# Windowed attention, soft routing and a feed-forward layer on one core: the last 64 tokens of every batch as two full-shaped units behind the others

## The chip, the cores and the metric

The kernel runs on one core of a Trainium2 chip. The metric is the device time of one execution in microseconds (us), lower is better. A time is given as the median of several executions. A profile is one execution recorded by the hardware profiler; its span runs from the first to the last instruction.

## The reference

Three layers follow each other, in float32, on 4 batches of 576 tokens (2304 tokens of 512 channels, 8 heads of 64):

```python
# 1. attention: each token sees itself and the 63 before it
mask = (rel >= 0) & (rel < 64)            # rel = query position - key position
attn = softmax(where(mask, q @ k.T / 8, -1e9))
x = (attn @ v)                            # -> (2304, 512)

# 2. soft routing: 8 experts x 4 slots, F = 1024
logits = x @ phi                          # (2304, 32)
d = exp(logits - logits.max(0)); d /= d.sum(0) + 1e-9    # over all tokens
slot_input = d.T @ x                      # (32, 512)
slot_out[e] = relu(slot_input[e] @ w1[e]) @ w2[e]
c = exp(logits - logits.max(1)); c /= c.sum(1) + 1e-9    # over the 32 slots
x = c @ slot_out

# 3. feed-forward, 2048 wide
h = x @ w_in
out = (h * sigmoid(1.702 * h)) @ w_out
```

## The kernel before

**Attention** is a software pipeline over a list `work` (L295). A unit is one pair of heads of one batch: 128 partitions hold the two heads, 64 channels each. The first 512 tokens of a batch, for one pair of heads, are a full unit (16 in all, `u`): four column blocks `c`, each of two chunks of 64 queries `j`, each chunk against 128 keys. The last 64 tokens of a batch, for all four pairs of heads together, are a half unit (4 in all, one per batch, standing second in its batch): two column blocks. So there are 20 steps `i`, in the order full, half, full, full, full for each batch.

A step (loop at L608) emits, for TensorE in this order: the scores of item i (`emit_s`: mask products L315, score products L329), the turn of the probabilities of item i-1 (`emit_t`, L350, copied to SBUF by ScalarE at L351), what the batch's routing has to do early, the turn of the attended rows of item i-2 (`xt_step`, L406 for a full unit, L412 for a half one), the value products of item i-1 (`emit_pv`, L365), and what routing has to do late. ScalarE computes the exponentials of a full item in two groups of four (`emit_e`, L341); VectorE takes the row maxima (L334) ahead of them and normalizes item i-1 behind the value products (`emit_norm`, L375 to L391).

**Routing** runs over batches as a running softmax over tokens, each batch 576 tokens in five tiles (four of 128 and one of 64, `TB`). For a batch it is spread over four steps: `logits` (L467, in two parts of 256 and 320 tokens), `lsum` (L480, two parts, four partial sums added by a product with a tiled identity), `lmax` and `dexp`, `dtr` (two turns of five blocks each, L510), `slots` (four products of 128 tokens, L527, and two of 64, L532), `gather` (running sum), and the softmax over slots (`c_max` to `c_mul`, on VectorE ahead of `emit_norm`). The last batch's routing stands behind the loop (L677 to L734) and ends with the 32 slot inputs turned (L731), which the expert layer waits for.

**Conversion** of six weight blocks that arrive as 64-bit words (`narrow_a` on ScalarE, `narrow_c` on GpSimd, `narrow_b` on VectorE, L169 to L177) is spread over steps 2 to 16; it stands at the end of a step.

**Loads** all go through one queue, SP's, in program order: q and k of a full unit (`load_qk`, 512 KB, three buffers), v (`load_v`, 256 KB, three buffers), the half unit's q, k and v of a batch (`load_sg`), and the expert weights (`load_w`, 1 MB each, 32 of them, one for each step from the third on, `W_AT`). The first 16 weight blocks go to buffers of their own, the next seven into the memory of the attention stage (`arena`) as it comes free, the last nine into buffers that the first expert products free. GpSimd scales q by 1/8 (`scale_q`, L218) and copies v for the second chunk (`shift_v`, L238, L241).

**Then** the expert layer (`emit_w1` L746, `emit_w2` L786) reads the 32 weight blocks, with the combine weights turned beside it (`c_last` for the four 64-token tiles, L448), and the feed-forward layer (L942 to L995) takes the rest of the span.

Of the kernel before, what the change touches and what calls it, by code (L numbers as in the profile page):

```python
# [32 lines left out]
W_AT = {i: 1 for i in range(2, 18)}  # L33
W_AT.update({18: 3, 19: 1})
# [8 lines left out]
TB = 5  # L43
# [7 lines left out]
SG0 = 0  # L51
X0 = SG0 + 4 * 192 + 517
QK0 = X0 + 2560
V0 = QK0 + 2048
MASK0 = V0 + 2 * 904
IDB0 = MASK0 + 512
XT0 = IDB0 + 64
LT0 = XT0 + 4 * S
D0 = LT0 + S
PHI0 = D0 + 160  # L60
X1 = PHI0 + 128
ARENA = 7 * 2048
N_E = 16
LS0 = NE * 260 + 512 - S

FP = 4

PERM = list(range(9))


def tw(t):
    return 128 if t < 4 else 64


@with_exitstack
def attention_softmoe_ffn(
# [4 lines left out]
    sg: bass.AP,  # L81
# [39 lines left out]
    lg = [cst.tile([128, TB, NS], F32, name=f"lg{b}") for b in range(B)]  # L121
# [4 lines left out]
    wof = cst.tile([128, N_WO, 512], F32, name="wof")  # L126

# [9 lines left out]
    plan += [(w2t, w2, i, 16 - N_E + i if i < N_E - 9 else None) for i in range(16)]  # L137
# [64 lines left out]
    vi = [v[:, 1:904].rearrange("p (i d) -> p i d", d=129) for v in vb]  # L202

    sgb = mem(SG0, 768).rearrange("p (u k) -> p u k", u=NHP)
    sgv = mem(SG0 + 768, 517)
# [3 lines left out]
    xb = [mem(o, 2560).rearrange("p (t d) -> p t d", t=TB) for o in (X0, X1)]  # L209
    xT = mem(XT0, KD * S).rearrange("p (k n) -> p k n", k=KD)  # L210
    lt = mem(LT0, S)
    phi4 = mem(PHI0, 128)

    def load_qk(u):
        nc.sync.dma_start(out=qkb[u % 3], in_=qk[u])

    def scale(q, eng):
# [3 lines left out]
    def scale_q(u, eng):  # L221
        scale(qkb[u % 3][:, 0:512], eng)

    def load_v(u):
        nc.sync.dma_start(out=vi[u % 3][:, 0:4, 0:128], in_=vt[u])

    def load_sg(b):
        nc.sync.dma_start(out=mem(SG0, 768), in_=sg[b, :, 0:768])
        nc.sync.dma_start(
            out=sgv[:, 1:517].rearrange("p (u d) -> p u d", u=NHP)[:, :, 0:128],  # L230
            in_=sg[b, :, 768:1280].rearrange("p (u d) -> p u d", u=NHP))

    def scale_sg(eng):
        scale(sgb[:, :, 0:64], eng)

    def shift_v(u):
        vd = vi[u % 3]
# [8 lines left out]
    for i in range(3):  # L246
        nc.vector.memset(vb[i][:, 0:1], 1.0)
        nc.vector.memset(vi[i][:, 0:4, 128:129], 1.0)
# [213 lines left out]
    def routing(b):  # L462
# [112 lines left out]
        def c_hi():  # L575
            c_high(b * S, st["pq"])
# [562 lines left out]
```

## Time and profile before

| | before |
|---|---|
| time, median of 3 executions (lowest to highest) | 387.69 us (387.28 to 388.26) |
| span of the profiled execution | 385.5 us |
| attention steps, first scores to the end of the loop's last full step | 6.4 to 104.2 us |
| turn, products and routing behind them, to the first expert product | 104.2 to 120.4 us |
| expert layer | 120.4 to 153.2 us |
| feed-forward layer to the end | 153.2 to 385.5 us |
| TensorE busy / ScalarE busy / VectorE busy (whole span) | 367.9 / 202.4 / 244.1 us |

The profile lists the busy time of each engine, the span in 40 equal slices, the groups of instructions by line, the chain of waits that ended last, and the instructions in order of time. PE is TensorE's matmul, PEld its weight load, DVE VectorE, ACT ScalarE, POOL GpSimd, SP the engine that issues the transfers. A float32 product shows as two records. A matmul's recorded duration overlaps with its neighbours', so the cost of a group on TensorE is read as the distance from its start to the start of the next group.

### The profile page before, as it was taken

The page shows a single profiled execution, that of the slowest core. Times are in us where ns is not written, and L with a number is a line of the kernel's source. Part 1 is how long each engine was busy: PE and PEld are TensorE (multiplying, and loading weights), DVE is VectorE, ACT ScalarE, POOL GpSimd, SP SyncE. Part 2 cuts the span into 40 slices and gives each one's busy share as a digit, 9 for nine tenths or more (in the row PEclk, how much of TensorE's full clock was granted, in tenths as well). Part 3 has the DMA queues.
Part 4 walks back from the last instruction along what each step waited for, and adds up shares of the span by engine and source line. Part 5 has one row for each costly group of instructions (what it writes and reads, how often), then busy time and mean ns, then how long its engine had stood idle before and what let it go on. Part 6 is the DMA issues. An engine that isn't in the chain of part 4 may idle for free.

```text
span 385.5 us, 7973 instructions
## 1 busy us (share of the span) xinstructions
PE 367.9 (95%) x3128; PEld 277.4 (72%) x3128; DVE 244.1 (63%) x554; ACT 202.4 (52%) x517; POOL 47.4 (12%) x79
## 2 busy tenths in 40 slices
PE   6999989889989999989999999999999999999995
PEld 5787667677654333768877888788887888888884
DVE  3466696896743540386677669597968795362624
ACT  2598868788742320556475745455444553343330
POOL 5335465343010000000000000000000000000000
PEclk9699999999999999999999999999999999999999
DMA  8999999999568999231413141313110000021304
GB/s 275 334 354 385 396 384 397 376 385 382 227 265 295 401 418 387 91 110 57 163 43 103 31 151 57 109 54 111 54 54 2 1 0 2 1 94 71 153 12 164
DMA packets 26726, 70.84 MB, mean 184 GB/s; under 512 B 2496, under 2 KB 13760, under 8 KB 22720
## 3 DMA queue, kind: packets, MB, share of 16 engines
q1 hardware_dynamic: 26688, 70.33, 49.3%
q8 instruction: 25, 0.41, 0.4%
q14 instruction: 13, 0.11, 0.1%
HBM read 65.60 MB, written 4.72 MB: 182 GB/s over the span
## 4 chain that ended last, share of the span: by engine, by line
PE 81%; DVE 9%; ACT 8%; issue 1%; POOL 0%; ACTq 0%
PE s L969 17%; PE t L969 16%; PE v L969 16%; PE m L942 4%; PE s L746 4%; PE v L786 4%; PE v L365 3%; PE s L329 3%; ACT pa L341 3%; PE m L350 3%; ACT pa L351 3%; DVE nm L334 1%; PE s L315 1%; PE v L256 1%; PE m L471 1%
## 5 line engine op out<-in xcount | busy, mean ns | idle before, releaser
L929 ACT ACTIVATE r<-m 128x384 fp32r<-128x384 f32 x96 | 47.3, 494 | 83.2 <-PE m L942 83.2
L956 DVE TENSOR_TENSOR r<-g,r 128x384 fp32r<-128x384 f32 x96 | 51.2, 553 | 50.6 <-ACT g L929 42.3
L969 PE MATMUL t<-w,r 128*128 128x512 f32 x288 | 75.9, 395 | 0.0
L969 PE MATMUL s<-w,r 128*128 128x512 f32 x288 | 74.9, 394 | 0.4 <-DVE r L956 0.4
L969 PE MATMUL v<-w,r 128*128 128x512 f32 x288 | 73.3, 389 | 0.0
L969 PEld LDWEIGHTS t<-w,r 128*128 128x128 f32 x288 | 53.8, 188 | 14.9 <-issue 3.7
L969 PEld LDWEIGHTS v<-w,r 128*128 128x128 f32 x288 | 54.1, 188 | 11.4
L969 PEld LDWEIGHTS s<-w,r 128*128 128x128 f32 x288 | 52.5, 188 | 9.5 <-DVE r L956 0.9
L341 ACT ACTIVATE pa<-s,nm 128x128 f32<-128x128 f32 x144 | 42.6, 401 | 11.7 <-DVE nm L334 11.6
L929 ACT ACTIVATE g<-m 128x384 f32<-128x384 f32 x96 | 47.7, 498 | 0.0
L334 DVE TENSOR_REDUCE nm<-s 128x4 f32<-128x512 f32 (+1 forms) x40 | 23.5, 629 | 6.0 <-PE s L329 5.8
L942 PE MATMUL m<-cT,w 128*128 128x384 f32 (+2 forms) x112 | 26.0, 322 | 0.6 <-ACT g L929 0.6
L351 ACT COPY pa<-m 128x512 f32<-128x512 f32 (+1 forms) x40 | 20.2, 563 | 9.9 <-PE m L350 9.6
L942 PEld LDWEIGHTS m<-cT,w 128*128 128x128 f32 x112 | 20.7, 188 | 5.8 <-ACT g L929 1.7
L350 PE MATMUL m<-ident,pa 128*128 128x128 f32 x144 | 21.8, 291 | 0.2 <-ACT pa L341 0.2
L350 PEld LDWEIGHTS m<-ident,pa 128*128 128x128 f32 x144 | 16.3, 145 | 4.5 <-issue 2.1
L365 PE MATMUL v<-arena,pa 128*64 128x65 f32 x384 | 15.9, 227 | 0.9 <-ACT pa L351 0.4
L365 PEld LDWEIGHTS v<-arena,pa 128*64 128x64 f32 x384 | 13.0, 137 | 4.2 <-ACT pa L351 2.9
L375 DVE TENSOR_SCALAR rs<-v 128x4 f32<-128x4 f32 (+1 forms) x40 | 5.2, 157 | 16.8 <-PE v L365 16.7
L746 PE MATMUL s<-w,phis 128*32 128x512 f32 x128 | 14.5, 594 | 0.5 <-DVE phis L734 0.5
L329 PE MATMUL s<-arena 64*64 64x128 f32 x384 | 14.7, 285 | 0.1
L315 PE MATMUL s<-arena 64*64 64x512 bf16 (+1 forms) x80 | 10.2, 397 | 3.7 <-ACT pa L341 3.0
(184 smaller groups left out, 461.0 us busy)
## 6 DMA issues: line engine op xcount, KB each, us to landing
w<-in_w_dram SPq DMA_DIRECT2D x24, 1024.0 KB, 10.4
w<-in_w_out_dram SPq DMA_DIRECT2D x16, 512.0 KB, 3.3
arena<-in_w_dram SPq DMA_DIRECT2D x7, 1024.0 KB, 6.9
iraw<-in_w_in_dram SPq DMA_DIRECT2D x12, 512.0 KB, 3.3
arena<-in_qk_dram SPq DMA_DIRECT2D x10, 512.0 KB, 8.7
out_dram<-w SPq DMA_DIRECT2D x16, 256.0 KB, 2.1
rawt<-in_qk_dram SPq DMA_DIRECT2D x6, 512.0 KB, 7.1
arena<-in_vt_dram SPq DMA_DIRECT2D x10, 256.0 KB, 7.4
```

The costliest lines, as they stand in the source:

```text
L329: nc.tensor.matmul(st[h][rows[j], c, :], q, k, start=False, stop=(c == n - 1), tile_position=(64 * h, 64 * j))
L334: nc.vector.tensor_reduce(out=nm[:, h, 0:n], in_=st[h][:, 0:n], axis=AX.X, op=ALU.max, negate=True)
L341: nc.scalar.activation(out=pb[h][:, c, :], in_=st[h][:, c, :], func=ACTF.Exp, bias=nm[:, h, c:c + 1], scale=1.0)
L350: nc.tensor.transpose(tt[:, c, :], pb[h][:, c, :], ident)
L351: nc.scalar.copy(ab[h][:, 0:n], tt[:, 0:n])
L365: nc.tensor.matmul(pvt[i][h][64 * j:64 * j + 64, c, :], ab[h][:, c, 64 * j:64 * j + 64], v, start=True, stop=True, tile_position=(0, 64 * j))
L746: nc.tensor.matmul(ph[32 * j:32 * j + 32, :], siT[:, kk, :], w1t[4 * r + j][:, kk, :], start=(kk == 0), stop=(kk == KD - 1), tile_position ...
L786: nc.tensor.matmul(po[32 * j:32 * j + 32, c], ht[:, e * 256 + fc * 32:e * 256 + fc * 32 + 32], w2t[i][:, j, c], start=(i == 0), stop=(i == ...
L929: nc.scalar.activation(out=(gh, g)[part], in_=ph[:, 0:PIECE], func=ACTF.Gelu_apprx_sigmoid)
L942: nc.tensor.matmul(ph[:, c - a:c - a + m], mst[:, f * 128:f * 128 + 128], cT(c, m), start=True, stop=True)
L956: nc.vector.tensor_tensor(out=gl, in0=g, in1=gh.bitcast(F32), op=ALU.subtract)
L969: nc.tensor.matmul(accs[t], a[:, c], b, start=(first and k == 0), stop=(last and k == 2))
```

## The change

The four half units go. In their place two tail units stand at the end of `work`, steps 16 and 17, each with the last 64 tokens of two batches: all four pairs of heads are its four column blocks, the two batches its two chunks, so a tail unit has a full unit's shape. A batch's own routing now covers 512 tokens in four tiles, in one part instead of two; the 256 tail tokens are a fifth routing group behind the loop, in two tiles (`xl`, `tail_logits`, `pd`, `pl`), whose logits are made in one accumulation with `phi4` in full (four blocks) instead of partial sums. The two turns of a batch share one bank. `gather` and the softmax over slots move behind `emit_norm` (`post`), the conversion's VectorE parts move to the middle of a step, `xt_step` ahead of the early routing. The loop has 18 steps; the last item's turn and value products stand behind it, among the last batch's `lsum`, `lmax`, `dexp`, `slots`. The tails' q and k come as four loads of 384 KB through the unit buffers, the last one into memory that the third batch's rows leave free. The arena is laid out anew and the seven weight blocks enter it in another order. The combine weights of the tails are turned as two full tiles; tokens lie in the order 4 x 512, then 4 x 64, and the host puts the rows back.

```diff
-W_AT = {i: 1 for i in range(2, 18)}
-W_AT.update({18: 3, 19: 1})
+W_AT = {i: 1 for i in range(2, 15)}
+W_AT.update({15: 1, 16: 1, 17: 2})
...
-    work = []
-    for b in range(B):
-        n = [(NHP * b + k, None) for k in range(NHP)]
-        work += n[0:1] + [(None, b)] + n[1:]
+    work = [(u, None) for u in range(NU)] + [(None, t) for t in range(2)]
...
+        def logits():
+            lp = bank("m")
+            for kk in range(KD):
+                nc.tensor.matmul(
+                    lp[32 * kk:32 * kk + 32], phis[:, kk, :], xT[:, kk],
+                    start=True, stop=True, tile_position=(0, 32 * kk))
+            nc.scalar.copy(lt, lp)
...
         def lsum():
+            lp = bank("m")
+            nc.tensor.matmul(lp, i4m, lt, start=True, stop=True)
+            nc.scalar.copy(ls, lp)
...
-                    start=True, stop=(t > 1), tile_position=(0, 32 * t))
-            for t in range(2):
-                cols = slice(256 * t, 256 * t + 256)
-                nc.tensor.matmul(
-                    pa[32 * t:32 * t + 32, cols], d[0:64, 4, :], x[0:64, 4, cols],
-                    start=False, stop=True, tile_position=(0, 32 * t))
+                    start=True, stop=True, tile_position=(0, 32 * t))
...
-        n = 5 * b
-        late[n + 6] = main[0:1]
-        early[n + 7] = main[1:2]
-        late[n + 7] = main[2:4]
-        early[n + 8] = main[4:5]
-        late[n + 8] = main[5:7] + norm[0:3]
-        late[n + 9] = norm[3:7]
+        n = NHP * b
+        late[n + 5] = [logits]
+        if b == B - 1:
+            break
+        early[n + 6] = [lsum]
+        late[n + 6] = [lmax, dexp]
+        early[n + 7] = [lambda f=turn: f(0, 1), total]
+        late[n + 7] = [slots]
+        post[n + 7] = [gather] + norm[0:2]
+        late[n + 8] = norm[2:3]
+        post[n + 8] = norm[3:7]
...
+    for i in range(ns):
+        emit_s(i)
         if i:
             emit_t(i - 1)
+        emit_e(i, 0)
+        convert(i, True)
+        if i > 1:
+            xt_step(i - 2)()
         for f in early.get(i, ()):
             f()
...
+        emit_e(i, 1)
         for f in late.get(i, ()):
             f()
         if i:
             emit_norm(i - 1)
+        for f in post.get(i, ()):
+            f()
...
+        if i < NU - 1:
+            scale_q(i + 1, nc.gpsimd)
+        elif i < NU + 1:
+            for n in range(2):
+                scale_q(NU + 2 * (i + 1 - NU) + n, nc.gpsimd)
...
+        if i == NU - 1:
+            set_ones(NL - 1, nc.gpsimd)
+            load_qk(NL - 1)
+            load_v(NL - 1)
...
+    load_w(2)
+    emit_t(ns - 1)
+    lsum()
+    xt_step(ns - 2)()
     sides[0][0]()
+    emit_pv(ns - 1)
+    lmax()
+    dexp()
+    emit_norm(ns - 1)
+    load_w(1)
     sides[0][1]()
...
+    turn(0)
+    tail_logits(0)
     xt_step(ns - 1, True)()
+    slots()
...
+    tail_logits(1)
...
+    nc.scalar.activation(
+        out=ltt, in_=lpt, func=ACTF.Exp, bias=m, scale=1.0, accum_out=ss)
...
+    for t in range(2):
+        nc.tensor.transpose(pd[:, t, :], ltt[0:32, t * 128:t * 128 + 128], ident[0:32, 0:32])
+    nc.vector.tensor_copy(dt, pd)
...
+            nc.tensor.matmul(
+                pl[32 * g:32 * g + 32, HALVES[c]], dt[:, t, :], xl[:, t, HALVES[c]],
+                start=True, stop=True, tile_position=(0, 32 * g))
...
-    c_last()
+    for f in side(TM, 4 * MT, "m"):
+        f()
```

## Rows read from the trace of the kernel before

**Rows 1.** The page, span in 40 slices of 9.64 us: granted clock and transfer rate.
```profile
PEclk9699999999999999999999999999999999999999
...
GB/s 275 334 354 385 396 384 397 376 385 382 227 265 295 401 418 387 91 110 57 163 43 103 31 151 57 109 54 111 54 54 2 1 0 2 1 94 71 153 12 164
```

**Rows 2.** Busy time by stretch: us, then each engine (records), clock, DMA share, GB/s.
```profile
63.17:89.18 26.01, 23.73 (x411) 17.58 (x407) 20.49 (x60) 19.82 (x60) 10.97 (x17) 1.00 1.02 383
...
109.52:120.38 10.86, 8.96 (x137) 5.99 (x134) 7.12 (x23) 3.75 (x11) 1.78 (x1) 1.00 0.54 189
120.38:153.17 32.79, 32.79 (x350) 11.91 (x350) 10.47 (x30) 6.34 (x15) 0.16 (x1) 1.00 1.01 398
```

**Rows 3.** TensorE in order of time: start us, us, line, out<-in, records [idle before, releaser].
```profile
62.04 1.20 PE L471 MATMUL m<-arena,phis 128*32 128x256 f32 x16
63.17 0.41 PE L315 MATMUL s<-arena 64*64 64x512 bf16 x4
...
64.38 0.66 PE L350 MATMUL m<-ident,pa 128*128 128x128 f32 x4
64.87 1.27 PE L480 MATMUL m<-arena,i 128*128 128x256 f32 x4
65.98 0.60 PE L406 MATMUL m<-ident,arena 128*128 128x128 f32 x4
66.51 0.69 PE L365 MATMUL v<-arena,pa 128*64 128x65 f32 x16
67.12 0.41 PE L315 MATMUL s<-arena 64*64 64x512 bf16 x4
...
68.34 1.09 PE L350 MATMUL m<-ident,pa 128*128 128x128 f32 x8
...
84.24 0.56 PE L315 MATMUL s<-arena 64*64 64x256 bf16 x4
...
85.21 1.15 PE L350 MATMUL m<-ident,pa 128*128 128x128 f32 x8
...
95.56 0.46 PE L510 MATMUL m<-ident,arena 32*128 32x32 f32 x5
...
96.61 0.66 PE L412 MATMUL m<-ident,arena 128*128 128x128 f32 x4
97.19 1.15 PE L365 MATMUL v<-arena,pa 128*64 128x65 f32 x32
98.28 1.06 PE L527 MATMUL m<-arena 128*32 128x512 f32 x8
99.27 0.62 PE L532 MATMUL m<-arena 64*32 64x256 f32 x4
99.83 0.41 PE L315 MATMUL s<-arena 64*64 64x512 bf16 x4
```

**Rows 4.** TensorE's waits, 20 to 110 us: us in total, times, longest.
```profile
PE m L406 <- DVE arena L385: 1.3, 3, 0.5
PE s L315 <- ACT pa L341: 1.1, 1, 1.1
```

**Rows 5.** The page's groups, the exponentials: count | busy, mean ns | idle before, releaser.
```profile
L341 ACT ACTIVATE pa<-s,nm 128x128 f32<-128x128 f32 x144 | 42.6, 401 | 11.7 <-DVE nm L334 11.6
```

**Rows 6.** TensorE in order of time, the scores of the third item, early.
```profile
15.55 1.78 PE L329 MATMUL s<-arena 64*64 64x128 f32 x32
```

**Rows 7.** TensorE in order of time, end of the routing and the last combine tiles.
```profile
117.27 0.62 PE L532 MATMUL m<-arena 64*32 64x256 f32 x4
...
118.83 1.08 PE L731 MATMUL m<-i,acc 128*128 128x32 f32 x8
...
137.69 1.08 PE L430 MATMUL t<-ident,lg 128*32 128x128 f32 x32
```

**Rows 8.** In order of time: SP issues q and k of a unit, GpSimd scales it.
```profile
76.19 0.33 SPq L215 DMA_DIRECT2D arena<-in_qk_dram  x1
...
83.58 0.62 POOL L218 TENSOR_SCALAR arena<-arena 128x512 f32<-128x512 f32 x1 [3.80 <-DMA arena<-in_qk_dram]
```

More of the change, by code (lines that the diff above doesn't have):

```diff
@@ L42 @@
 NT = B * S
-TB = 5
+TM = 4
+MT = 128 * TM
 MASKED = -1.0e9
@@ L136, in attention_softmoe_ffn @@
     plan = [(w1t, w1, i, None if i < N_E else i - N_E) for i in range(16)]
-    plan += [(w2t, w2, i, 16 - N_E + i if i < N_E - 9 else None) for i in range(16)]
+    plan += [(w2t, w2, i, (0, 2, 3, 1, 4, 5, 6)[i] if i < 7 else None) for i in range(16)]
     plan.reverse()
@@ L339, in emit_e @@
         st, nm = est[i]
-        for c in range(shape_of(i)):
+        for c in range(4):
             nc.scalar.activation(
@@ L416, in evac @@
-        def evac():
-            if split:
-                nc.scalar.copy(o[:, HALVES[0]], ps[0])
-                nc.vector.tensor_copy(o[:, HALVES[1]], ps[1])
-            else:
-                nc.scalar.copy(o, p)
+        ps = [pt[:, c] for c in HALVES]
+        if split:
+            ps[1] = bank("m")[:, HALVES[0]]
+        for k in range(4):
+            if t is None:
+                b, kk = divmod(u, NHP)
+                src = xb[b % 2][:, k, kk * 128:kk * 128 + 128]
+            else:
+                src = xl[:, t, k * 128:k * 128 + 128]
+            nc.tensor.transpose(ps[k // 2][:, 128 * (k % 2):128 * (k % 2) + 128], src, ident)
@@ L422, in xt_step @@
+        def evac():
+            if t is None:
+                nc.scalar.copy(xT[:, kk], pt)
+                return
+            o = xlT[:, :, 128 * t:128 * t + 128]
+            if not split:
+                nc.scalar.copy(o, pt.rearrange("p (k n) -> p k n", k=KD))
+                return
+            for k, copy in ((0, nc.scalar.copy), (2, nc.vector.tensor_copy)):
+                copy(o[:, k:k + 2], ps[k // 2].rearrange("p (k n) -> p k n", k=2))
         return evac
-    PARTS = ((0, 256), (256, S))
@@ new lines, in attention_softmoe_ffn @@
+    nc.vector.tensor_scalar(out=rsl, in0=rsl, scalar1=1e-9, scalar2=None, op0=ALU.add)
+    nc.vector.reciprocal(out=rsl, in_=rsl)
+    i4s = cst.tile([128, NS], F32, name="i4s")
+    nc.vector.tensor_scalar(
+        out=i4s, in0=i4m[:, 0:NS], scalar1=rsl, scalar2=None, op0=ALU.mult)
+    siT = phis
+    sides[2][0]()
+    psi = bank("m", (128, KD, 32))
+    for k, c in enumerate(HALVES):
+        p = slice(64 * k, 64 * k + 64)
+        nc.vector.tensor_tensor(out=acc[p, c], in0=pl[p, c], in1=acc[p, c], op=ALU.add)
+        for kk in (2 * k, 2 * k + 1):
+            nc.tensor.matmul(
+                psi[:, kk, :], acc[:, kk * 128:kk * 128 + 128], i4s, start=True, stop=True)
@@ L772, in attention_softmoe_ffn @@
     emit_ht(1)
-    for f in sides[3]:
+    for f in side(0, 3 * MT, "m"):
         f()
```

470 lines of the change are left out of this document (197 added, 273 removed).

## Prediction

> **What bounds the kernel now.** I read the span by stretches first [rows 2]. In one batch of the attention loop (five steps, 26.0 us) TensorE is busy for 23.7 us, VectorE for 20.5, ScalarE for 19.8: TensorE sets the pace, with 2.3 us of gaps, but ScalarE is not far behind. The expert layer is TensorE alone: 32.8 of 32.8 us. The feed-forward layer behind it is not touched (the order of the tokens changes, not the tiles' shapes), so only attention, routing and the expert layer can move. Transfers come next [rows 1]: 376 to 397 GB/s from the fourth to the tenth slice, then a dip, then 400 again: the first 96 us stream without a pause, and the question is whether a shorter loop overtakes its loads. The granted clock falls to 6 tenths in the second slice alone [rows 1]. Then I read TensorE in order of time [rows 3], taking the distance from one start to the next as a group's cost, and last its waits [rows 4].
>
> **Half units to tail units.** From [rows 3]: a half unit's scores take 85.21 - 84.24 = 0.97 us, its turn of probabilities 64.87 - 64.38 = 0.49, its turn of rows 97.19 - 96.61 = 0.58, its value products 67.12 - 66.51 = 0.61: 2.65 us, four times 10.60. A full unit costs 68.34 - 67.12 = 1.22 for scores, twice 0.49 for the turn, 66.51 - 65.98 = 0.53 for rows, 98.28 - 97.19 = 1.09 for value products: 3.82. Two tail units have its shapes: 7.64. The turn and score groups cost nearly as much for two column blocks as for four, so joining two saves. **-3.0 us**, all on TensorE, which has next to no gap in which it could have been hidden.
>
> **Routing of the first three batches.** 512 columns for 576 and one part for two: logits 63.17 - 62.04 = 1.13, times 512/576 = 1.00; lsum 65.98 - 64.87 = 1.11, becomes 0.99; the two turns 96.61 - 95.56 = 1.05 for ten blocks, 0.84 for eight; slots loses its second part, 99.83 - 99.27 = 0.56 [rows 3]. That is 1.0 us a batch, **-3.1 us**. ScalarE and VectorE lose their second copies and the 64-row pieces with it; I count nothing for them here.
>
> **The first steps.** The second step was a half unit and becomes a full one, in the stretch at half clock. At that clock 32 score products take 1.78 us [rows 6], the same group some 1.0 later. Half a unit's scores, turn and value products, about 1.2 us at full clock, stand where they cost twice: between 0 (the wait for the first exponentials there hides part) and +1.2; I take **+0.6 us**.
>
> **Behind the loop.** Before the last value products, TensorE now has the whole of the last batch's logits and lsum (1.00 + 0.99 us, where three quarters of the logits stood, 0.85) and the first combine turn, moved forward (1.0 for 32 records [rows 7]): +2.1. The 1.0 leaves the next stretch, where it is hidden today, so it is paid here; but the turn of the last probabilities, which now follows a step without scores and waits for its exponentials, gets the logits ahead of it as cover. I give that and what else overlaps an estimate of -1.4, between 0 and -2.1. **+0.7 us.** Behind the last value products lie 10.86 us now [rows 2], a serial chain: normalize, turn, logits, maximum, exponential, turn, slots, sum, turn. On the tails alone it has one exponential and one maximum of 256 columns instead of two each (-0.9, about two ScalarE and VectorE operations of 0.4 to 0.5), and the product behind the exponential is 0.56 us like slots' second part instead of 1.55 for both parts (99.83 - 98.28) [rows 3]: -1.0. From slots' second part to the last turn pass 118.83 - 117.27 = 1.56 us [rows 7]; the rescaling is now split over `i4s` and may add 0.2. The last batch's own slots (0.99) are queued on TensorE ahead of the second tail's logits, while the turned rows are copied: +0.1 for what outlasts that copy. Sum **-1.6 us**, between 0 and -2.5.
>
> **Expert layer.** The combine turns of four 64-token tiles become two full ones: 32 records take 1.08 us [rows 7], 16 half of it; the last batch's turn has six blocks for five, +0.1. **-0.4 us**, as TensorE has no gap there [rows 2].
>
> **Waits.** The 2.3 us of gaps a batch [rows 2] have two kinds of row: the turn of rows waits for VectorE's normalizing (1.3 us in all) and a score product waits for a bank that ScalarE's late exponentials hold (1.1) [rows 4]. Both are late because VectorE has the routing's softmax ahead of normalizing, and conversion ahead of the next maxima. The change moves the first behind and the second to where VectorE waits for the value products anyway: this can give back up to all 2.3 us a batch, 6.8 in three. Against it: every step is now a full one for ScalarE. A full unit's exponentials are 8 x 42.6/144 = 2.4 us [rows 5], and 19.8 us a batch of four such units and a half one [rows 2] leave some 4 for a full step with its copies and its share of routing. Steps that also convert and carry lsum and the batch's exponential need more than TensorE's time; by about 1.0 us in one step of four, I estimate. The half units were where ScalarE caught up. Bounds: -4.3 (nearly two thirds of the gaps) to +3.0 (that 1.0 each batch, nothing gained). I take **-1.5 us**, nearer the middle of them than the good end, because the chain rows show VectorE's lateness only in two steps of a batch.
>
> **Transfers.** The bytes up to the sixteenth weight block are the same (about 35 MB), in about the same time: at the end of my step 8 some 19.7 MB are asked for and, by [rows 1], about 18 delivered; by step 15 delivery has caught up. So nothing is added. The weight blocks for the arena are issued in step with what the routing frees, as before, and the nine behind them wait for expert products as before; they move ahead with the loop. Cover lost would show as gaps in the expert layer.
>
> **Sum.** -3.0 - 3.1 + 0.6 + 0.7 - 1.6 - 0.4 - 1.5 = -8.3. The profiled span is 385.5, so the new span would be 377.2; 2.2 us lie between span and median, so 387.69 - 8.3 = **379.4 us**. Own range of this case: 376.4 to 383.
>
> **A new load late in the loop.** The last tail's q and k are issued only after the third batch's slots have been read (step 15), scaled by GpSimd in step 16 and needed at the start of step 17, some 4 us after the issue. SP is in order, so the last v and the weight blocks 14 to 16 queue behind it. At 76.19 us a load of this kind was issued that GpSimd got at 83.58, 7.4 us later, but behind queued weight blocks [rows 8]. By my count little is queued at step 15, and 384 KB at 390 GB/s are 1.0 us. [...] The row of 7.4 us speaks for the queue as the larger part.
>
> **Rivals.** (1) ScalarE takes over: with only full steps, waits grow by the +3.0 instead of falling by 1.5. Time 379.4 + 4.5 = 383.9. For it speaks its 19.8 us busy a batch, of which only some 2 go with the half unit (four of its exponentials are 1.2) while the batch shrinks by about 4; against it, that the heavy step is followed by a step heavy for TensorE (turns and slots). (2) Slower: the late load above. From 4 us after its issue each us of delay is a us of TensorE's idle time; at 7.4 us it costs 3.4 (382.8); from 12.3 the whole gain is gone; at 14 the kernel is at about 389.4. For it: the loop is shorter and weight blocks come one a step, so the queue may hold two of them more than I count, and TensorE's clock could fall in so long a gap. Against it: it needs nearly twice the delay that the row shows. (3) No change: the half steps' TensorE time was cover for ScalarE and VectorE, and what TensorE saves is given back as waits everywhere: 387.7. Against it stands 23.7 us busy of 26.0. (4) Faster still: the granted clock is down in the second slice, which begins in the second step, where a score product waits for the first exponentials. If a full unit there keeps it at its upper level (2.4 GHz, not 1.2), the group of 1.78 us becomes 1.05 and its neighbours likewise, some 3 us: 376.4. The Trainium skill ("TensorE: Matmul & The Clock Gate", section "Part 1: The HAM clock gate") says that an idle stretch throttles the engine and sustained work releases it; the trace agrees (6 tenths in the second slice, 9 behind it), and by it this rival needs the gap to go. I see no reason for that: the same first exponentials end it.
>
> **How the numbers follow.** Chances: forecast 0.60, (1) 0.22, (2) 0.06, (3) 0.06, (4) 0.06. The range of 8 in 10 takes in the forecast's own and most of (1) and (4): 376.2 to 384.8. A measurement of this kernel tells about 0.3% (1.2 us) from no change. Faster by more: the forecast, (1) and (4), 0.88; within: 0.06; slower: 0.06.
>
> **What would show it.** In the profile after: the first expert product near 112.5 us instead of 120.4; a batch in four steps of together 21 to 21.5 us, with under 2 us of gaps on TensorE; from the last value products to the first expert product near 9.3 us; the expert layer still without a gap, 32.4 us long. Rival (1) shows as waits of the turn of probabilities or of a score product for ScalarE, 1 us and more in the lsum step; (2) as a wait of a score product for GpSimd at the start of step 17; (3) as batches of 25 us; (4) as a clock of 9 in all slices. Wrong would be the prediction above all if the gaps grow, since that term alone is an estimate of sign as well as size; the others are records that are no longer there.

## The result and the profile after

The changed kernel takes 375.14 us (median of four runs, 374.26 to 375.5) against 387.98 us for the kernel before, measured in turn with it. The ratio is 0.967, with a 95% interval of 0.962 to 0.972: 12.8 us faster, where 8.3 was forecast, and just under the low end of the range. The profiled span goes from 385.5 to 373.3 us, that is 12.2 less. The direction was right, the sizes of several terms were not; this section and the next ones look for the 4 us that came on top (4.5 by the medians, 3.9 by the spans).

The page of the changed kernel, granted clock and transfer rate in 40 slices of 9.33 us (compare [rows 1]):

```profile
PEclk9999999999999999999999999999999999999999
...
GB/s 237 338 387 392 388 393 391 388 361 317 420 419 421 420 391 277 56 114 112 59 112 56 103 67 113 58 86 83 114 0 0 2 0 0 2 122 48 138 34 169
```

The 6 in the second slice is gone, and the dip of 227 and 265 GB/s in the eleventh and twelfth slices has shrunk to one slice of 317.

Busy time by stretch of the changed kernel, columns as in [rows 2]. The stretches are the second and third batch, the one from the end of the loop to the end of the last value products, the one from there to the first expert product, and the expert layer:

```profile
26.39:46.84 20.45, 20.05 (x349) 14.74 (x347) 15.41 (x40) 17.04 (x51) 10.70 (x13) 1.00 1.04 391
46.84:67.78 20.94, 20.34 (x352) 14.72 (x348) 17.26 (x48) 17.70 (x54) 11.65 (x16) 1.00 1.05 390
95.86:100.32 4.46, 4.46 (x80) 3.46 (x79) 1.05 (x4) 3.63 (x9) 0.00 (x0) 1.00 1.02 419
100.32:109.27 8.95, 8.00 (x117) 5.92 (x116) 6.06 (x24) 2.96 (x9) 1.83 (x1) 1.00 1.02 421
109.27:141.71 32.44, 32.44 (x335) 11.55 (x335) 10.58 (x23) 6.12 (x11) 0.00 (x0) 1.00 1.02 411
```

Against [rows 2]: a batch takes 20.5 to 20.9 us instead of 26.0, and TensorE stands still for 0.4 and 0.6 us of it instead of 2.3. From the last value products to the first expert product it is 8.95 us instead of 10.86, and the expert layer takes 32.44 instead of 32.79, still without a gap. So the largest change is in the loop, and it is twofold: fewer records, and fewer gaps. (A wait inside a group, as in the logits below, counts as busy in these rows.)

TensorE in order of time in the changed kernel: the second step (first three lines), and the second batch (the rest):

```profile
9.67 0.40 PE L312 MATMUL s<-arena 64*64 64x512 bf16 x2 [1.76 <-ACT pa L339]
9.78 1.17 PE L327 MATMUL s<-arena 64*64 64x128 f32 x32
10.88 1.09 PE L347 MATMUL m<-ident,pa 128*128 128x128 f32 x8
...
30.44 1.60 PE L448 MATMUL m<-arena,phis 128*32 128x512 f32 x8
31.97 0.41 PE L312 MATMUL s<-arena 64*64 64x512 bf16 x4
...
34.37 0.60 PE L400 MATMUL m<-ident,arena 128*128 128x128 f32 x4
34.82 1.12 PE L457 MATMUL m<-arena,i 128*128 128x512 f32 x2
35.88 1.15 PE L362 MATMUL v<-arena,pa 128*64 128x65 f32 x32
```

Three readings. The second step still waits 1.76 us for the first exponentials (before: 1.86), but the full unit behind it then runs its 32 score products in 1.17 us, not in the 1.78 of [rows 6]. The logits, one part now, take 31.97 - 30.44 = 1.53 us where I had 1.00: the last quarter's weights wait for ScalarE's copy of the turned rows. And lsum takes 35.88 - 34.82 = 1.06, where I had 0.99.

ScalarE and TensorE's weight load (PEld) ahead of and in these logits, in order of time:

```profile
29.31 1.16 ACT L339 ACTIVATE pa<-s,nm 128x128 f32<-128x128 f32 x4
...
30.32 0.62 ACT L404 COPY arena<-m 128x512 f32<-128x512 f32 x1
...
31.00 0.14 PEld L448 LDWEIGHTS m<-arena,phis 128*32 128x32 f32 x2 [0.40 <-ACT arena L404]
```

The copy stands behind four exponentials of a full unit (1.16 us). In the kernel before, a half unit stood in that step: two exponentials (0.64 us), the copy from 35.33 to 35.94, and logits from 36.21 to 37.32 that didn't wait for it. In the next two batches of the changed kernel the logits take 1.85 and 1.86 us.

TensorE's waits in the changed kernel from 20 to 110 us, columns as in [rows 4]:

```profile
PE s L327 <- POOL arena L236: 1.2, 1, 1.2
PE m L400 <- DVE arena L381: 0.6, 2, 0.3
PE s L735 <- DVE phis L716: 0.5, 1, 0.5
```

The two waits of [rows 4] are answered by the second line: the turn of rows waits for VectorE 0.6 us in all instead of 1.3, and the wait of a score product for ScalarE's exponentials (1.1) is not in the list. New is the first line, which is the late load of the last tail's q and k. In order of time, SP, GpSimd and TensorE of the changed kernel:

```profile
84.66 0.33 SPq L228 DMA_DIRECT2D arena<-in_sq_dram  x1
...
90.00 0.40 POOL L236 TENSOR_SCALAR arena<-arena 128x256 f32<-128x256 f32 x1 [1.86 <-DMA arena<-in_sq_dram]
...
90.46 0.32 PE L327 MATMUL s<-arena 64*64 64x128 f32 x1 [1.22 <-POOL arena L236]
```

From issue to GpSimd 5.3 us pass, between the 1.0 that I took and the 7.4 of [rows 8].

### The profile page after: what moved, and what is told of

Read it like the earlier page. It is cut to its first block, busy times and chain, and to the rows that moved or that the text cites. A ratio compares the mean times of both kernels' runs of the same rounds, so it can differ in the third digit from the quotient of the medians.

```text
span 373.3 us, 7763 instructions
## 1 busy us (share of the span) xinstructions
PE 359.9 (96%) x3060; PEld 271.9 (73%) x3060; DVE 238.4 (64%) x520; ACT 200.1 (54%) x501; POOL 45.8 (12%) x74
## 4 chain that ended last, share of the span: by engine, by line
PE 82%; ACT 9%; DVE 5%; DMA 1%; issue 1%; POOL 0%; ACTq 0%
PE s L959 17%; PE t L959 17%; PE v L959 17%; PE m L932 4%; PE s L735 4%; PE v L776 4%; ACT pa L348 3%; PE v L362 3%; ACT pa L339 3%; PE s L327 3%; PE m L448 2%; PE m L347 2%; DMA arena<-in_sq_dram 1%; PE v L264 1%; PE m L507 1%
## 5 line engine op out<-in xcount | busy, mean ns | idle before, releaser
L332 DVE TENSOR_REDUCE nm<-s 128x4 f32<-128x512 f32 x36 | 23.1, 683 | 9.7 <-PE s L327 9.4
L348 ACT COPY pa<-m 128x512 f32<-128x512 f32 x36 | 19.5, 600 | 13.8 <-PE m L347 13.8
L347 PE MATMUL m<-ident,pa 128*128 128x128 f32 x144 | 19.7, 280 | 0.0
L347 PEld LDWEIGHTS m<-ident,pa 128*128 128x128 f32 x144 | 15.4, 141 | 3.8 <-issue 2.2
L327 PE MATMUL s<-arena 64*64 64x128 f32 x368 | 12.9, 269 | 1.2 <-POOL arena L236 1.2
L381 DVE TENSOR_TENSOR arena<-v,rs 128x256 f32<-128x256 f32 x36 | 13.6, 418 | 0.6
L904 ACT CAST w<-wf 128x512 fp32r<-128x512 f32 x14 | 8.7, 622 | 9.1 <-DVE wf L175 9.1
```

The costliest lines, as they stand in the source:

```text
L327: nc.tensor.matmul(st[h][rows[j], c, :], q, k, start=False, stop=(c == 3), tile_position=(64 * h, 64 * j))
L332: nc.vector.tensor_reduce(out=nm[:, h], in_=st[h], axis=AX.X, op=ALU.max, negate=True)
L347: nc.tensor.transpose(tt[:, c, :], pb[h][:, c, :], ident)
L348: nc.scalar.copy(ab[h], tt)
```

## The experiments

What was open: is the extra gain in the moves of the gather, the softmax and the conversion behind normalizing, put down as part of "waits" at 1.5 us; in TensorE's clock, charged with 0.6 us; or in a term of the records? Medians below stand beside those of the kernel before of the same comparison, which lie between 387.1 and 387.7 us unless they are given.

### The kernels again

Both kernels unchanged.

> The kernel before, unchanged, profiled a second time. Theory A (the clock's fall in the second slice belongs to the program: its second step is a half unit behind a pause): the granted clock is at half between about 10 and 17 us again, the first expert product comes at 120.4 us, span 385.5. Theory B (the fall is a matter of chance, of the moment at which the run starts): the clock may stay up, and then the first expert product comes about 3 us earlier.

> The changed kernel, profiled a second time. Theory A: the granted clock stays at its upper level from the first scores on, first expert product at 109.3 us, span 373.3. Theory B: the clock may fall in the first 20 us here too, and the span is then about 3 us longer.

> The changed kernel unchanged, for the spread of its executions. The kernel before spreads from 385.4 to 391.0 us in 19 runs, and its profiles show the clock falling at another place each time (10 to 17, 10 to 13, in a sibling 118 to 126 us). If the changed kernel leaves no pause in which the clock falls, its runs stay within about 1 us (374.2 to 375.5); if it is a matter of chance, they spread over 4 us or more as well.

Measured: 385.85 us for the kernel before (span 384.1), and 374.91 and 375.24 us (374.33 to 377.29 in four runs) for the changed one, spans 373.0 and 372.8. Busy time by stretch of the kernel before in this second execution, 10 to 14 and 14 to 18 us:

```profile
10.00:14.00 4.00, 3.74 (x48) 2.89 (x43) 0.76 (x2) 2.45 (x8) 2.87 (x6) 0.59 1.08 373
14.00:18.00 4.00, 3.86 (x82) 3.01 (x81) 3.23 (x12) 2.27 (x9) 0.71 (x2) 1.00 1.03 405
```

The granted clock, the third number from the right, is 0.59 for four microseconds and 1.00 behind them; the execution that I predicted from has 0.53 and 0.62 in the same two stretches. Its first row:

```profile
10.00:14.00 4.00, 3.74 (x40) 2.89 (x40) 0.76 (x2) 2.63 (x9) 2.77 (x5) 0.53 1.07 376
```

The group of [rows 6] takes 1.05 us here instead of 1.78, and the first expert product starts at 118.89 instead of 120.38. So 1.5 us of the execution on which I predicted were its longer stretch at 1.2 GHz, not a property of the kernel.

The mean granted clock of every execution says how often this happens. Of 68 executions of the kernel before, five have 0.998 or more, and these take 385.4 to 386.5 us (median 385.6); the median of all is 387.4. Of nine executions of the changed kernel eight have it (median 375.0), and the ninth, with 0.995, takes 377.29. So some 1.8 us of the median of the kernel before are the clock, and the changed kernel loses it too, but more rarely.

### The clock, from the side of the kernel before

The half unit one step later, so that the second step is a full one:

```diff
-        work += n[0:1] + [(None, b)] + n[1:]
+        work += n[0:2] + [(None, b)] + n[2:]
```

> The kernel before with the half unit third instead of second in every batch; nothing else is moved, the amount of work is the same. Theory A: the second step is then a full unit as in the changed kernel, the clock doesn't fall, and the kernel is faster by about 3 us (384.7). Theory B, or a fall that hangs on the pause alone: no change, 387.7, clock at half as before.

Measured: 387.67 us (385.88 to 391.19, ten runs), ratio 1.002 (0.998 to 1.005). The early fall is gone in the profiled execution, but another came. Its page, the granted clock in 40 slices of 9.74 us:

```profile
PEclk9999999999995999999999999999999999999999
```

and its busy time by stretch, early and where the clock falls:

```profile
14.00:18.00 4.00, 3.92 (x81) 3.31 (x80) 2.19 (x10) 3.57 (x13) 0.87 (x2) 1.00 1.02 360
116.00:120.00 4.00, 4.00 (x49) 2.48 (x41) 1.79 (x6) 0.59 (x1) 0.00 (x0) 0.62 0.56 170
120.00:124.00 4.00, 3.52 (x18) 1.55 (x21) 0.29 (x1) 0.00 (x0) 0.00 (x0) 0.50 0.95 363
```

It runs at half level among the short pauses at the end of the routing and into the expert layer. A full second step is therefore no cure in itself: my first reading, that the half unit in the second step is what lets the clock fall, is not borne out.

Then products that do nothing, in the early pause (eight, between the scores of items 0 and 1), and in a second kernel also two at each of four places behind the loop:

```diff
+        if i == 1:
+            for _ in range(8):
+                nc.tensor.matmul(bank("v")[:, 0:128], ident, ident, start=True, stop=True)
...
+    warm(2)
```

> The kernel before with eight idle products (128 x 128 x 128, result unused) on TensorE between the scores of the first and of the second item, where it pauses for 1.86 us. If the pause makes the clock fall, it stays up and the kernel is faster by about 3 us (384.7). If the light second step behind the pause makes it fall, it falls all the same, and the time is 387.7 or a little above.

> The kernel before with idle products in both pauses of TensorE: eight between the first two items' scores and four times two behind the loop. If the spread of the kernel before (385.4 to 391.0 us) is the clock falling in one pause or the other, this one stays within about 1.5 us and its median is about 385.5, 1.5 to 2 us under the kernel before; if the spread has another source, it stays at 387 with the same spread.

Measured: 386.99 us (385.01 to 390.38, ten runs; ratio 0.999, 0.995 to 1.002) with the first eight, 386.51 (385.23 to 388.14, twelve runs; ratio 0.996, 0.994 to 0.999) with both, and a granted clock of 1.00 in both profiles. So the idle products are worth 1.1 us of the median, and they narrow the spread (the kernel before reached from 386.5 to 392.2 beside it). They don't keep the clock up each time: 8 of the 12 executions with both sets have a mean clock of 0.998 or more, and these take 386.2, still 0.6 above the kernel before at that clock. That not more arrives is seen in TensorE's order of time with the first eight products:

```profile
31.44 0.67 PE L329 MATMUL s<-arena 64*64 64x128 f32 x16 [1.23 <-POOL arena L218]
```

What is won early is waited for at the second half unit, whose q GpSimd has not scaled yet.

### The clock, from the side of the changed kernel

One product that needs the last exponentials of item 0, ahead of the scores of item 1, so that the pause is longer:

```diff
+        if i == 1:
+            nc.tensor.matmul(bank("v")[:, 0:128], pb[1][:, 3, :], ident, start=True, stop=True)
```

> The changed kernel with its pause in the second step made longer: one idle product that needs the first item's last exponentials stands ahead of the second item's scores, so TensorE waits some 1.2 us more there. The delay alone costs 1.0 to 1.2 us (376.3). If a pause of this length is what makes the clock fall, some executions lose 1.5 to 3 us on top, and the spread grows to 3 us or more.

Measured: 377.95 us (375.99 to 380.58), ratio 0.972 (0.966 to 0.978). TensorE in order of time:

```profile
10.50 0.80 PE L596 MATMUL v<-ident,pa 128*128 128x128 f32 x2 [3.00 <-ACT pa L339]
11.22 0.64 PE L312 MATMUL s<-arena 64*64 64x512 bf16 x4
11.65 1.92 PE L327 MATMUL s<-arena 64*64 64x128 f32 x32
13.50 1.97 PE L347 MATMUL m<-ident,pa 128*128 128x128 f32 x8
```

Behind a pause of 3.00 us the scores take 1.92 us and the turn 1.97, against 1.17 and 1.09 above; the granted clock was 0.50 from 10 to 18 us. This is one of two outcomes: two of the four executions have a mean clock of 0.986 and take 379.4 and 380.6 us, the other two have 0.999 and 1.00 and take 376.5 and 376.0. The longer pause alone costs about 1.1 us, a fall some 3.7 on top of it, and a pause of this length doesn't bring the fall each time.

### The places, alone and undone

In the changed kernel, the gather, the softmax and the conversion back in their old places; and in the kernel before, those moves alone:

```diff
-        late[n + 7] = [slots]
-        post[n + 7] = [gather] + norm[0:2]
-        late[n + 8] = norm[2:3]
-        post[n + 8] = norm[3:7]
+        late[n + 7] = [slots, gather] + norm[0:3]
+        late[n + 8] = norm[3:7]
...
-        convert(i, True)
...
+        convert(i, True)
```

```diff
-        late[n + 8] = main[5:7] + norm[0:3]
-        late[n + 9] = norm[3:7]
+        late[n + 8] = main[5:6]
+        post[n + 8] = main[6:7] + norm[0:2]
+        late[n + 9] = norm[2:3]
+        post[n + 9] = norm[3:7]
...
```

> The changed kernel with gather, the softmax over slots and the conversion's VectorE parts back in their old places of a step (the softmax ahead of normalizing, the conversion at the step's end). Theory A (most of the gain is records that are gone; the moves give back some waits): slower than the changed kernel by 1.5 to 2.5 us, 376.6 to 377.6. Theory B (the moves are the larger part of what the prediction missed): slower by 4 us and more, 379 and up. Theory C (the moves give nothing): 375.1.

> The kernel before with those moves alone. Theory A: faster by about 1.5 us (386.0), since TensorE's gaps of 2.3 us a batch shrink by a third. Theory B: faster by 4 us and more (383.5). Theory C: 387.5.

> The kernel before with the same idle products and with gather, softmax and conversion in the places that the changed kernel gives them. If clock and places are two separate terms, they add: 2.9 from the places (384.2 measured for these alone) and 1 to 2 from the clock, together about 382.7 to 383. What is then left to the changed kernel, some 7.5 us, is the tail units and the four tiles. If both are the same gain twice, it stays at 384.

Measured: the changed kernel with the old places 377.74 us (376.21 to 378.52), 2.5 above the median of the changed one; the kernel before with the new places 384.24 (382.94 to 385.4, ten runs; ratio 0.992, 0.989 to 0.995), 2.9 below; with the idle products as well 384.07 (383.62 to 384.98), which is 2.4 below the same products without the moves (386.51). TensorE's waits, 20 to 110 us, of the changed kernel with the old places:

```profile
PE m L400 <- DVE arena L381: 2.3, 5, 0.8
PE s L312 <- ACT pa L339: 0.9, 3, 0.3
```

Where the changed kernel has 0.6 us for the first and nothing for the second, it now has 3.2: the wait of the turn of rows for normalizing is back, five times. The clock has to be kept apart here: the profiled execution with old places had it at 0.62 from 10 to 14 us, so of its 3.2 us of longer span about 1.6 are clock (its third item starts 15.12 - 9.56 = 5.56 us behind the second, against 13.66 - 9.67 = 3.99). The pair with idle products has 1.00 in both profiles, and it is the one that I go by: the moves are worth 2.4 us.

Two things limit this. On top of the new places the idle products add next to nothing (384.24 to 384.07), as the last sentence of the third expectation has it: the gains overlap, and -1.1 and -2.4 hold in this order only. And in the profile of the kernel before with the new places the wait for normalizing is down to 0.4 us from 1.3, but the score product's wait for ScalarE is still 1.0, and one of 1.4 for GpSimd's scaling of q is new; that the second wait of [rows 4] is gone is seen in the changed kernel alone. The move of `xt_step` ahead of the early routing is in neither pair and was not tested.

### The late load

The last tail's q and k in a place that is free earlier (the turned rows of the tails), with its load issued ahead of the slots of the third batch:

```diff
-    qlast, vlast = mem(X0, 768), mem(X0 + 768, 517)
+    qlast, vlast = mem(XLT0, 768), mem(X0 + 768, 517)
...
+        if i == NU - 1:
+            load_qk(NL - 1)
...
-            load_qk(NL - 1)
```

> The changed kernel with the last tail's q and k in memory that is free all along, so that their load is issued before the third batch's slots are read instead of behind them. The profile shows TensorE waiting 1.22 us for GpSimd's scaling of them. If that wait is on the path: 373.9, and the first expert product at 108.0 us; if ScalarE's exponentials are late there anyway: 374.6 to 375.1.

> The changed kernel with the last tail's load issued earlier, in more rounds: 374.2 to 374.5 against 375.2 if the 0.6 to 1.2 us of waiting seen in two profiles were on the path.

Measured: 374.35 us (373.62 to 378.83, four runs), and 375.35 (374.27 to 376.23, six runs), against 375.14 and 375.24 for the changed kernel. The wait for GpSimd is gone from the list, and the time is the same. TensorE's groups in order of time, and its waits behind 110 us, show where it went:

```profile
92.63 2.03 PE L448 MATMUL m<-arena,phis 128*32 128x512 f32 x8
```

```profile
PE v L777 <- DMA w<-in_w_dram: 0.6, 1, 0.6
```

The last logits, 1.60 us long in the changed kernel at 94.33, take 2.03 here, and the expert layer, reached at 108.00 us instead of 109.27, now waits 0.6 us for a weight block. The late load costs TensorE 0.6 to 1.2 us and the kernel nothing that can be measured.

### One part or two

The changed kernel with its logits and lsum in two parts of 256 columns:

```diff
-            lp = bank("m")
...
-            nc.scalar.copy(lt, lp)
+            for c in HALVES:
+                lp = bank("m")[:, 0:256]
...
+                nc.scalar.copy(lt[:, c], lp)
...
```

> The changed kernel with logits and lsum of a batch in two parts of 256 columns instead of one of 512, as many columns in all. By TensorE's records nothing changes but some 0.1 us a batch; two more banks are taken and two more copies of ScalarE are made a batch. If one part matters: slower by 1 us or more (376.2 and up), which would be what the prediction missed in the routing; if not, 375.2 to 375.6.

Measured: 377.06 us (374.05 to 377.94, four runs), ratio 0.971 (0.964 to 0.978): 1.8 us above the changed kernel by the medians, but the interval takes in both nothing and more than 3 us. Its waits:

```profile
PE s L327 <- POOL arena L236: 1.7, 1, 1.7
PE m L449 <- ACT arena L404: 1.0, 2, 0.7
```

The second line answers the longer logits of the changed kernel: in two parts it is a wait between groups, in one part it lies inside the group. So the wait for the copy belongs to the logits in either form, and the single part is not what brings it. The first line has a price of its own: behind it the granted clock was 0.50 from 92 to 94 us. Three of the four executions have a mean clock of 0.994; the fourth, at 1.00, takes 374.05, no more than the changed kernel. So the 1.8 us are the clock's, as far as one execution shows it, and not the second part's.

### The half units taken out

The kernel before without its half units, with its five tiles in two parts kept; once with the old places and once with the new ones. The weight blocks are issued one a step in steps 2 to 15 and six in step 16:

```diff
-W_AT = {i: 1 for i in range(2, 18)}
-W_AT.update({18: 3, 19: 1})
+W_AT = {i: 1 for i in range(2, 16)}
+W_AT.update({16: 6})
...
-        work += n[0:1] + [(None, b)] + n[1:]
+        work += n
...
```

> The kernel before without its four half units: the attention of the last 64 tokens of every batch is left out (zeros stand for their rows) with its loads; 16 steps, routing spread over a batch's four full steps, still five tiles in two parts, and the turn of the 64-token tile still made. Priced by records (scores, turn and value products of a half unit, 0.97 + 0.49 + 0.61, four times) it is 8.3 us faster: 379.3. If a half unit costs more than its records (its exponentials, maxima and normalizing delay the full units), it is 10 us and more: 377 and under. If half units were cover for ScalarE and VectorE, less than 8: above 380.

> The kernel before with the gather and the conversion of w1 in their new places, and without its half units: the attention of the last 64 tokens of every batch is left out (a part of the computation that this run does not do); five tiles in two parts stay. The kernel before with the new places alone has 384.2 us; the half units have records of 8.3 us. Theory A (a half unit costs its records and nothing more, and the old places were what made it seem cheaper): 376 us, first expert product near 110 us, no wait in the loop above 1.5 us in sum. Theory B (the half units' products are cover for ScalarE and VectorE also with the new places): about 379 to 380 us, with waits of 2 to 3 us for the raw rows or the transposed pairs in the loop. Theory C (the weight blocks, of which one waits for the last conversion, bind as soon as the loop is shorter): the loop ends near 110 us but the expert layer waits 2 us or more for a transfer of w, and the time is 378 to 380 us.

Measured: 384.08 us (382.39 to 386.45, ten runs; ratio 0.990, 0.986 to 0.995) in the old places, which is 3.4 us below the kernel before of that comparison (387.47); 375.92 us (375.24 to 376.32, four runs; ratio 0.970, 0.968 to 0.972) in the new ones, which is 8.3 us below the kernel before with the new places (384.24). The records that the half units have are 8.3 us. In the new places the time falls by as much; in the old ones most of it came back.

That the two agree to a tenth is in part luck. At a mean clock of 0.998 or more the kernel before with the new places takes 383.1 us (four of its ten executions), which leaves 7.2 of the 8.3. In the profiles the stretch from the first scores to the first expert product is 8.5 us shorter (101.98 against 110.44), although 3.0 us of waits in it come from the edit itself (below), and the expert layer is 1.2 longer (34.02 against 32.79). So a half unit costs about its records, and in the loop perhaps more.

TensorE's waits in the old places, from 20 to 110 us (first two lines) and from 110 to 150 (third):

```profile
PE m L403 <- ACT rawt L486: 3.0, 3, 1.0
PE m L411 <- DVE arena L383: 2.9, 4, 1.7
...
PE v L791 <- DMA w<-in_w_dram: 3.4, 3, 1.4
```

and in the new places, from 20 to 110 us (first two lines) and from 110 to 375 (third):

```profile
PE m L403 <- ACT rawt L486: 3.0, 3, 1.0
...
PE m L411 <- DVE arena L383: 0.4, 1, 0.4
...
PE v L798 <- DMA w<-in_w_dram: 0.8, 1, 0.8
```

The first line is the same in both and comes from the edit itself (it turns the fifth tile's rows in a place of its own); a removal without it was not run. The wait of the turn of rows for normalizing falls from 2.9 to 0.4 us, and the wait of the expert layer for weights from 3.4 to 0.8. The latter has its cause on SP, in order of time, in the old places:

```profile
80.51 23.76 SPq L147 DMA_DIRECT2D w<-in_w_dram  x5
```

and the wait costs more than itself, as the busy time by stretch in the expert layer of the same kernel shows:

```profile
142.00:146.00 4.00, 1.51 (x16) 0.31 (x16) 0.00 (x0) 0.00 (x0) 0.00 (x0) 1.00 0.99 409
146.00:150.00 4.00, 3.11 (x16) 0.35 (x12) 0.00 (x0) 0.00 (x0) 0.00 (x0) 0.52 1.07 370
```

SP stood for 23.76 us at a group of weight loads. By its list of waits 21.0 us of this are one wait for VectorE's last conversion step (L177, into `wof`), which frees a buffer; in the new places, with conversion earlier in the step, that wait is 13.6. Behind the pauses of 1.06 and 1.43 us that this made in the expert layer the clock was at 0.52. In this profiled execution, the slowest of the ten, the expert layer takes 39.5 us instead of 32.8, which is more than the 6.0 that the loop and the routing behind it had gained (106.51 against 112.50 in the second execution of the kernel before). So in the old places much of the gain was lost here, and not in the loop. That the conversion's place alone moves the weights was not run by itself, since the moves were made together.

## Why the prediction was right or wrong

The sum failed first of all at the step that I priced by one execution's clock: +0.6 us for the first steps, where the clock gave back 1.1 to 1.8 in the runs. The experiments cut the change in four. The mean clock is 0.998 or above in the profile of each kernel below the first, though not in every execution behind its median:

| step | median us | change | forecast |
|---|---|---|---|
| before | 387.6 | | |
| clock kept up (idle products) | 386.5 | -1.1 | +0.6 |
| new places on top | 384.1 | -2.4 | -1.5 |
| no half units (384.24 to 375.92) | 375.9 | -8.3 | -8.3 by records |
| tail units, routing in 512 columns, end | 375.1 | -0.8 | +0.9 |

The forecast of the last line is 8.3 - 3.0 = 5.3 for the tail units, -3.1, +0.7, -1.6 and -0.4. The four changes sum to -12.6, the forecasts to -8.3: of the 4.3 us, 1.7 lie in the clock, 0.9 in the places, 1.7 in the last line. Taken from the executions with a mean clock of 0.998 or more, and without idle products, the four changes are -1.8 (387.4 to 385.6), -2.5 (383.1), -7.2 (375.9) and -0.9 (375.0): the clock weighs more, the half units less.

**Half units to tail units, right.** The -3.0 rest on group durations taken as TensorE's pace, and the run without half units in the new places gives 8.3 for 8.3 by the medians (7.2 at equal clock, with 3.0 us of waits of its own). The condition under which it holds was not in my text: in the old places the same edit gave 3.4. My rival of no change ("the half steps' TensorE time was cover") was in good part right for that order of work, though much came back as a wait for weights and a lowered clock, and wrong for the changed one.

**Routing of three batches, mis-sized.** By the starts of its groups the routing of three batches gives back 1.1 us, not 3.1 (1.7 with a wait of 0.65 inside one of the old turns). Logits are 1.53 to 1.86 us, not 1.00, since I scaled a row by its columns (512/576) and did not ask what the last quarter's weights wait for: ScalarE's copy, now behind four exponentials where a half unit had two. Here the half unit was cover for ScalarE, which my text says of the waits and not of this term. The turn is 0.6 (I had 0.84), slots 1.0 as said, lsum 1.06 (0.99).

**The first steps, wrong.** The step that failed is the bound "between 0 and +1.2". I took the 1.78 us of [rows 6] as the price of this place and gave the clock no way to be up there ("I see no reason for that"; chance 0.06). The second execution of the kernel before shows 1.05 us for the same group, and both levels follow one and the same pause: 1.86 us of waiting end in a granted clock of 0.53 in one kernel and 1.00 in another, 1.75 in 0.62 and 1.00 (rows in the last section). In place of a fixed price stands one that some executions pay, and against +0.6 the clock gave 1.1 (idle products) to 1.8 us (executions with the clock up). What lowers its share in the changed kernel stays open: its profiles show the clock up in all three executions, its sibling with the early load shows it at 0.62 from 10 to 14 us in one of two, and a pause made longer by 1.2 us brings the fall in two executions of four. A mean clock of 0.998 or more have 5 of 68 executions of the kernel before, 3 of 10 with the half unit one step later, 4 of 10 with the new places and 8 of 9 of the changed kernel; the share grows with each of these edits, and so few executions don't say why. The gap did not need to go, which is where my sentence on the Trainium skill ("TensorE: Matmul & The Clock Gate", section "Part 1: The HAM clock gate") led me: it says that an idle stretch throttles and sustained work releases. The rows agree on both effects, and the 3.00 us pause shows the first; they don't support reading from it that a pause of a given length, here 1.8 us, settles the matter.

**Before the last value products, wrong; behind them, right.** The first expert product starts 102.94 us behind the first scores (109.27 - 6.33), in the run without half units 101.98 (108.36 - 6.38): the tail units, the shorter routing and the end together cost 1.0 us there, where my terms without the expert layer give 1.3. In the stages it is less even: the stretch ahead of the last value products fell from 5.28 to 4.46 us where I had +0.7, because I let only 1.4 of the 2.1 us overlap, with no row for it; the longer logits (2.2 us over three batches) and the late load's 1.2 us, ahead of it, took back more than that. That 1.0 comes near 1.3 is therefore a sum of misses, and the run that it is read against has 3.0 us of waits of its own. Behind the last value products it fell by 1.9 (forecast 1.6).

**Expert layer, right** (-0.35 for -0.4). Behind it the feed-forward layer took 231.59 us instead of 232.33, where I had nothing; TensorE's busy time there is 0.24 lower, and the rest I could not place. It was not tried, but it is no spread: all eight profiles of kernels made from the changed one have 231.5 to 231.6 us there, all nine of kernels made from the kernel before 232.1 to 232.4. The last line's 1.7 us are therefore some 0.5 of this (the run without half units in the new places has 232.12), 0.8 of the weight wait that this run has and the changed kernel has not, and a remainder of the size of the spread.

**Waits, right in kind, mis-sized.** "This can give back up to all 2.3 us a batch" is near what the profile shows: 0.4 and 0.6 us of gaps a batch remain, and some 0.5 and 0.9 more inside the logits. The two waits of [rows 4] are 2.4 us in all from 20 to 110 us, not 2.3 a batch; I read them as the kinds of all the gaps. I took -1.5 as "nearer the middle", for fear of ScalarE; the moves alone are 2.4, and without half units they are worth more, since both the turn of rows and the weights wait for VectorE's place in the old order. Rival (1), ScalarE as the bound, did not come: 17.0 and 17.7 us busy in batches of 20.5 and 20.9; its lateness shows in the logits alone.

**Transfers and the late load, right.** The load takes 5.3 us instead of 4 of cover and TensorE waits 0.6 to 1.2 us, in line with the rival's arithmetic, and not with its price: earlier, the same time (though in the run with two parts the clock fell behind a wait of 1.7 us there). "So nothing is added" holds for the changed kernel, with little to spare: 1 us sooner, a weight block is late by 0.6.

**The range** failed by how it was put together. I held the forecast and rival (4) against each other, as if the clock could only be up instead of the waits falling further. They add: 376.4 for the clock, and from there up to 2.8 for the waits at their good end, reach 373.6.

## What to carry to other kernels

A group of records is worth its duration only if the work that it covered has another place; ask of each engine's in-order queue what stands ahead of the instruction that the others wait for, and price the moves and the removal together, since here the removal alone gave 3.4 us, the moves alone 2.4 to 2.9, and both 11.2 (375.92 against 387.11). Look into a long group before calling an engine busy: the logits waited inside theirs. A row at a lowered clock is one execution's row: take a second execution before it becomes a price, and add, don't oppose, rivals that can come true together.

## What the runs showed of the hardware that was not expected

The same pause had two outcomes. Second step of TensorE in order of time: the kernel before with the new places, whose granted clock was 1.00 from 10 to 18 us:

```profile
9.09 0.30 PE L315 MATMUL s<-arena 64*64 64x256 bf16 x2 [1.86 <-ACT pa L341]
```

the kernel before as first profiled, where it was 0.53 from 10 to 14 us:

```profile
9.83 0.30 PE L315 MATMUL s<-arena 64*64 64x256 bf16 x2 [1.86 <-ACT pa L341]
```

and one and the same kernel, the changed one with the early load, whose clock was 1.00 the first time and 0.62 the second:

```profile
9.37 0.40 PE L312 MATMUL s<-arena 64*64 64x512 bf16 x2 [1.75 <-ACT pa L339]
```

```profile
9.55 0.60 PE L312 MATMUL s<-arena 64*64 64x512 bf16 x2 [1.75 <-ACT pa L339]
```

The changed kernel itself has 1.76 us and 1.00. In the kernels with the usual pause such an early fall lasted from 4 to 8 us and cost 1.2 to 2.7 us. And a queue that stands at one load holds back all behind it: 23.76 us on SP in the kernel without half units and with old places, of which 3.4 us reached TensorE, 60 us later.
